# Full-height score products with masked queries, O normalised by DMA and the B branch in chunks, in a fused attention and MLP kernel

## Chip, cores, metric

One core of a Trainium2 chip. The metric is the device time of one execution in microseconds (us), and the number quoted for a kernel is the median of all its runs; ratios use fast runs alone. A run is called slow when it lies over 1.5% above the fastest of the same kernel. The kernel before varies; its profiled run took 1158.88 us, 8 us above its median.

## What is computed

A layer-normed input goes through attention with 32 heads of 20, and through a gated MLP branch (B). The two are multiplied, and the input is added.

```python
x  = A_x                                   # (1, 2048, 640) bf16
xn = layernorm(x)
# A: 32 heads, Dh = 20
q, k, v = split(xn @ wqkv)
s = softmax(q k^T / sqrt(20)) v @ wo
# B
h  = shift4(gelu(layernorm(xn) @ w1)) @ w2   # four column groups shifted by 1, -1, 2, -2 rows
x1 = xn + h
b  = x1 + gelu(layernorm(x1) @ w3) @ w4
out = x + s * silu(b)
```

## The kernel before

The program is a list of tasks with estimated durations. A static list scheduler (the "planner") simulates the engines with these estimates and writes one fixed order per engine. Afterwards every engine works its list strictly in order and waits on semaphores.

```python
self.dma_bw = 280.0          # planner: bytes per ns, shared by all DMAs
self.dma_lat0 = 1900.0       # planner: ns from issue to landing, plus bytes / dma_bw
...
t.start = st
t.finish = st + t.dur
if t.is_dma and t.nbytes:
    xs = max(t.finish, dma_free)
    dma_free = xs + t.nbytes / self.dma_bw
    t.lat = dma_free + self.dma_lat0 - t.finish
```

Attention works in "groups": four heads (a quad) times 512 queries, 32 groups in all. A head occupies 32 partitions. Scores of two heads are two *row tiles*, which stream side by side (in the trace of before the two of a pair start 3 ns apart, at 861.420 and 861.423 us, and take 385 ns each). ScalarE takes the exp of both (128x1024), and a product with V in four *column tiles* adds into one PSUM bank. Some key tiles are done by VectorE's own exp instead. Two 2-bank areas hold ScalarE's scores, one bank holds PV (the product with V; its row Z is the sum of the exps, by which the output is divided), and three further banks ("W") serve everything else: VectorE's scores, the B branch, projections and transposes.

```python
def score(e, out, i):                       # row tile: 21 of 128 rows
    return e.matmul(out, KT[32*i:32*i+21, b, 128*kt:128*kt+128], QT[32*i:32*i+21, b, q0:q0+512],
                    start=True, stop=True, tile_position=(32*i, 0))
# ... ScalarE's tiles
T("pe", 240, fn, ...); T("act", c_act(1024), ... e.activation(PT[:, slot, :], psum..., AF.Exp, scale=cfg.scale) ...)
# ... VectorE's tiles: scores into W banks
T("pe", 130, fn, reads=krd + qrd, writes=[wa, ("dseq",)], acq=("W", h))

def normalise(self, quad, qc):              # O^T sits in PSUM with Z in row 20 of each 32
    T("dve", ..., lambda e: e.transpose(Ot[:, :], self.bank(self.PVB)[:, :]))
    T("dve", ..., lambda e: e.reciprocal(RZ[:, ob, 0:16], Ot[:, 20:512:32]))
    T("dve", ..., fnn)                      # OnT = Ot * RZ, one factor per row and block of 32
    T("dve", ..., lambda e: e.transpose(OT[:, 512*qc:512*qc+512], OnT[:, ob, :]))

def run_b(self, quad):                      # the B branch is filler: TensorE takes it only
    self.cur_cls = 1                        # when nothing of attention is ready
    for want, stage in self.b_stages:
        if want == quad:
            stage()
    self.cur_cls = 0
```

## Time and profile before

| | before |
|---|---|
| time, median of 3 (range) | 1150.85 us (1143.3 to 1166.96) |
| first exp starts, last exp ends, end | 42.4, 1087.3, 1156.9 us |
| ScalarE busy / idle from first to last exp | 862.7 / 182.2 us |
| granted TensorE clock, mean | 0.816 |
| time at clock 0.50, summed over the trace | 427 us |

The profile is read in this order: ScalarE's exps are the largest block of work that cannot be given away, so the span is the time before the first exp (head), ScalarE's busy and idle time from first to last exp, and the time after it (tail). The busy shares, slices, stretches and the order of time stand in the prediction. What ScalarE waited for before the change (line waited for: us in total, times, longest us):

```profile
ACT arena L1087 <- PE psum L1071: 128.1, 201, 5.8
ACT arena L1383 <- DVE arena L1379: 41.9, 3, 24.0
ACT arena L1302 <- DVE arena L1296: 32.0, 1, 32.0
```

Between first and last exp stand the 201 small waits for score products and one large one, before a gelu (L1302), for VectorE's part of the B branch. The three before a silu (L1383) lie in the tail, but for 0.2 us. VectorE appears in no wait of an exp.

### The profile page before, as it was taken

The page shows a single profiled execution, that of the slowest core. Times are in us where ns is not written, and L with a number is a line of the kernel's source. Part 1 is how long each engine was busy: PE and PEld are TensorE (multiplying, and loading weights), DVE is VectorE, ACT ScalarE, POOL GpSimd, SP SyncE. Part 2 cuts the span into 40 slices and gives each one's busy share as a digit, 9 for nine tenths or more (in the row PEclk, how much of TensorE's full clock was granted, in tenths as well). Part 3 has the DMA queues.
Part 4 walks back from the last instruction along what each step waited for, and adds up shares of the span by engine and source line. Part 5 has one row for each costly group of instructions (what it writes and reads, how often), then busy time and mean ns, then how long its engine had stood idle before and what let it go on. Part 6 is the DMA issues. An engine that isn't in the chain of part 4 may idle for free.

```text
span 1156.9 us, 27991 instructions
## 1 busy us (share of the span) xinstructions
PE 1047.0 (90%) x12648; PEld 332.8 (29%) x12648; DVE 768.5 (66%) x1328; ACT 895.2 (77%) x914; POOL 30.8 (3%) x52
## 2 busy tenths in 40 slices
PE   4999999999779999999779999999989899989896
PEld 3422222222223332223221222123222233233374
DVE  6656677467447788676866687576787858843355
ACT  7589798688529899788847798688999989988700
POOL 3010000000000000000000000000010000000000
PEclk9978696598659899678855696587999889978999
DMA  4110000000110001000030001010021100200231
GB/s 114 10 32 6 1 5 5 2 1 1 9 43 2 2 2 8 2 2 1 5 85 1 7 13 20 13 29 2 1 48 41 25 2 19 47 7 8 52 117 59
DMA packets 85486, 24.53 MB, mean 21 GB/s; under 512 B 74360, under 2 KB 85368, under 8 KB 85368
## 3 DMA queue, kind: packets, MB, share of 16 engines
q1 hardware_dynamic: 85368, 22.75, 9.1%
q8 instruction: 99, 1.62, 0.6%
q14 instruction: 19, 0.16, 0.0%
HBM read 19.99 MB, written 2.62 MB: 20 GB/s over the span
## 4 chain that ended last, share of the span: by engine, by line
PE 74%; ACT 18%; DVE 5%; DMA 1%; issue 1%; POOL 0%; SPq 0%; DVEq 0%
PE psum L687 28%; PE psum L1071 25%; ACT arena L1087 15%; PE psum L1096 10%; PE psum L1144 9%; ACT arena L1370 1%; PE psum L908 1%; DVE arena L845 1%; DMA arena<-in_B_w_dram 1%; DVE arena L1296 1%; ACT arena L1383 1%; DVE arena L1121 1%; PE psum L944 0%; DVE arena L1227 0%; DMA arena<-in_A_x_dram 0%
## 5 line engine op out<-in xcount | busy, mean ns | idle before, releaser
L1087 ACT ACTIVATE arena<-psum 128x1024 bf16<-128x1024 f32 x844 | 818.4, 1028 | 155.6 <-PE psum L1071 128.1
L1071 PE MATMUL psum<-arena 21*128 21x512 bf16 x2048 | 419.5, 443 | 45.6 <-ACT arena L1087 37.3
L687 PE MATMUL psum<-arena 128*32 128x320 bf16 (+1 forms) x6480 | 421.4, 376 | 29.2 <-DVE arena L1296 7.5
L1134 DVE TENSOR_SCALAR arena<-arena 128x2048 uint16<-128x2048 uint16 x360 | 230.8, 689 | 42.0 <-PE psum L1144 40.8
L687 PEld LDWEIGHTS psum<-arena 128*32 128x32 bf16 x6480 | 161.7, 102 | 199.7 <-issue 84.3
L1124 DVE TENSOR_SCALAR arena<-psum 128x512 uint16<-128x512 f32 x266 | 170.4, 682 | 62.7 <-PE psum L1071 61.9
L1071 PEld LDWEIGHTS psum<-arena 21*128 21x128 bf16 x2048 | 91.7, 93 | 391.2 <-ACT arena L1087 224.5
L1096 PE MATMUL psum<-arena 128*22 128x512 bf16 x1688 | 191.1, 445 | 3.3 <-DVE arena L1158 3.3
L1144 PE MATMUL psum<-arena 128*22 128x512 bf16 x1440 | 135.5, 462 | 0.6 <-POOL arena L1048 0.6
L1096 PEld LDWEIGHTS psum<-arena 128*22 128x22 bf16 x1688 | 42.0, 90 | 128.2 <-issue 118.9
L1121 DVE TENSOR_SCALAR arena<-psum 128x1024 uint16<-128x1024 f32 x47 | 57.2, 1217 | 20.8 <-PE psum L1071 20.6
L1366 DVE CAST arena<-psum 128x512 bf16<-128x512 f32 x48 | 33.0, 689 | 41.3 <-PE psum L687 41.1
L1144 PEld LDWEIGHTS psum<-arena 128*22 128x22 bf16 x1440 | 36.8, 100 | 53.9 <-issue 41.7
L1383 ACT ACTIVATE arena<-arena 128x1280 bf16<-128x1280 bf16 x8 | 10.2, 1270 | 41.9 <-DVE arena L1379 41.9
L1158 DVE STREAM_TRANSPOSE arena<-psum 128x512 f32<-128x512 f32 x32 | 22.9, 715 | 24.9 <-PE psum L1096 24.5
L1296 DVE CAST arena<-psum 128x512 bf16<-128x512 f32 x20 | 13.8, 691 | 36.2 <-PE psum L687 36.2
L987 DVE TENSOR_SCALAR arena<-psum,arena 128x512 bf16<-128x512 f32 x32 | 23.7, 744 | 20.0 <-PE psum L687 19.9
L1379 DVE TENSOR_TENSOR arena<-psum,arena 128x320 bf16<-128x320 f32 x32 | 15.0, 488 | 32.6 <-PE psum L687 32.6
L908 PE MATMUL psum<-arena 128*32 128x128 bf16 x640 | 24.7, 276 | 10.1 <-DVE arena L918 5.8
L1302 ACT ACTIVATE arena<-arena 128x5120 bf16<-128x5120 bf16 x2 | 8.9, 4470 | 32.0 <-DVE arena L1296 32.0
L918 DVE COPY arena<-psum 128x512 bf16<-128x512 bf16 x40 | 16.8, 420 | 20.8 <-PE psum L908 20.7
L1327 DVE TENSOR_TENSOR arena<-psum,arena 128x320 bf16<-128x320 f32 x32 | 15.7, 489 | 19.6 <-PE psum L687 19.6
(70 smaller groups left out, 338.7 us busy)
## 6 DMA issues: line engine op xcount, KB each, us to landing
arena<-in_B_w_dram SPq DMA_DIRECT2D x48, 160.0 KB, 2.4
arena<-in_A_x_dram SPq DMA_DIRECT2D x8, 320.0 KB, 5.7
arena<-in_A_x_dram SPq DMA_DIRECT2D x16, 160.0 KB, 2.3
out_dram<-arena SPq DMA_DIRECT2D x16, 160.0 KB, 2.2
arena<-in_B_w_dram SPq DMA_DIRECT2D x1, 1920.0 KB, 8.3
arena<-in_A_wqkv_dram SPq DMA_DIRECT2D x64, 25.0 KB, 2.5
arena<-in_B_w_dram SPq DMA_DIRECT2D x2, 800.0 KB, 4.7
arena<-in_A_wqkv_dram SPq DMA_DIRECT2D x2, 400.0 KB, 6.5
```

The lines of the kernel that those rows point to most:

```text
L687: ins = e.matmul(pb[32 * c:32 * c + 32, 0:N], lhsT(k, c), rhs(k, c), start=(k == 0), stop=(k == nk - 1), tile_position=(0, 32 * c))
L908: ins = e.transpose(pb[32 * c:32 * c + 32, 128 * bi:128 * bi + 128], src_of(n)[:, kc * 128 + 32 * c: kc * 128 + 32 * c + 32], self.ident[: ...
L987: T("dve", c_dve(512), lambda e, h=h, c0=c0: e.tensor_scalar(KT[:, b, c0:c0 + 512], self.wbank(h)[:, 0:512], self.eaug[:, 0:1], None, op0= ...
L1071: return e.matmul(out, KT[32 * i:32 * i + 21, b, 128 * kt:128 * kt + 128], QT[32 * i:32 * i + 21, b, q0:q0 + 512], start=True, stop=True, ...
L1087: lambda e, sb=sb, slot=slot: e.activation(PT[:, slot, :], self.psum[:, 1024 * sb:1024 * sb + 1024], AF.Exp, scale=cfg.scale),
L1096: ins = e.matmul(pb[32 * i:32 * i + 22, 0:512], VA[:, ql, kt, i, :], PT[:, slots[i // 2], 512 * (i % 2):512 * (i % 2) + 512], start=first, ...
L1121: return e.tensor_scalar(dst, self.psum[:, 512 * (self.W0 + lo):512 * (self.W0 + hi + 1)], a_exp, EXP_BIAS, op0=ALU.mult, op1=ALU.add)
L1124: ins = e.tensor_scalar(dst[:, 512 * k:512 * k + 512], self.bank(self.W0 + s)[:, :], a_exp, EXP_BIAS, op0=ALU.mult, op1=ALU.add)
L1134: lambda e, s=s, v=v: e.tensor_scalar(SS[:, s, :], U[:, :], 0.5, EXP_B[v], op0=ALU.mult, op1=ALU.add),
L1144: ins = e.matmul(pb[32 * i:32 * i + 22, 0:512], w, SS[:, s, at:at + 512].bitcast(BF16), start=first and v == 0, stop=final and v == 3, til ...
L1296: T("dve", c_dve(512), lambda e, h=h, m=m, ch=ch: e.tensor_copy(hx[:, m, 512 * ch:512 * ch + 512], self.wbank(h)[:, 0:512]), reads=[wa], w ...
L1366: T("dve", c_dve(512), lambda e, h=h, fc=fc: e.tensor_copy(GT[:, fc, :], self.wbank(h)[:, 0:512]), reads=[wa], writes=at, name=f"gt_{ch}_{ ...
```

## The change

The intent: fewer switches between row tiles and column tiles on TensorE (about 0.10 us each from start to start in the kernel before) and a fuller array; less VectorE work in normalising; no B-branch rest after the last exp.

```diff
+# scores for ScalarE: four column tiles of 128 rows on queries that are zero outside one head
+T("sp", 240, lambda e: [e.dma_start(self.QM[32*i:32*i+32, gb, i, :], QT[32*i:32*i+32, b, 512*qc:512*qc+512]) for i in range(4)], ...)
+for c in range(4):
+    ins = e.matmul(bank[32*c:32*c+32, :], self.KT[:, b, 128*kt+32*c:128*kt+32*c+32],
+                   self.QM[:, gb, 2*a+jj, :], start=True, stop=True, tile_position=(0, 32*c))
+# row tiles stay in "blocks" of two key tiles that ScalarE and VectorE share: BLK = [(4,5),(9,10),(14,15)]
+# planner: a task has a tiling mode; a change costs 100 ns, and tasks of the same mode are taken first

 def normalise(self, quad, qc):
-    transpose, reciprocal, multiply, transpose          # four VectorE steps
+    T("dve", ..., lambda e: e.tensor_copy(Ob[:, :], self.bank(self.PVB)[:, :]))
+    T("sp", 240, fz, ..., ndma=4)      # Z: one row -> 32 partitions x 16, four heads
+    T("dve", ..., lambda e: e.reciprocal(RZ[:, ob, :], ZT[:, ob, :]))
+    T("sp", 240, fb, ..., ndma=4)      # 1/Z back into one row
+    T("sp", 240, fc, ..., ndma=4)      # that row to 19 further partitions: [[..],[0,19],[1,512]]
+    T("dve", ..., lambda e: e.tensor_tensor(dst, Ob[:, :], RB[:, :], op=ALU.mult))
+    T("sp", 60*len(moves), fd, ...)    # into O packed to 5 x 128 rows
+    # (the very last group keeps the transposes)

-# B branch: y2, w1, w2 over all 2048 rows, as filler (cls 1)
+# B branch: per chunk of 512 rows (y2 is its normalised input, RR the factor of each row), in the foreground (cls 0); ScalarE's scores get cls -1
+T("sp", 60, lambda e: e.dma_start(RR[1:128, :], bass.AP(..., [[..],[0,127],[1,S]])))   # row scale to 127 partitions
+T("dve", ..., fy)                      # y2 chunk = xnT * RR, waits for all of RR
```

Cut from the diff: row tiles of 32 rows instead of 21, bookkeeping for several DMAs under one semaphore, the tables of which group shares how many blocks, the output projection on five packed K tiles, memory layout. The planner has 60 ns for each DMA issue in all of it.

## The prediction

> **What bounds the kernel now.** I read the page's busy shares first, then its slices, then stretches, then the order of time at small scale, and last the waits.
>
> ```profile
> PE 1047.0 (90%) x12648; PEld 332.8 (29%) x12648; DVE 768.5 (66%) x1328; ACT 895.2 (77%) x914; POOL 30.8 (3%) x52
> ...
> PEclk9978696598659899678855696587999889978999
> ...
> L1087 ACT ACTIVATE arena<-psum 128x1024 bf16<-128x1024 f32 x844 | 818.4, 1028 | 155.6 <-PE psum L1071 128.1
> ```
>
> TensorE is busy 90% of the span, but its granted clock swings between 5 and 9 tenths. ScalarE, which must do 844 exps, sits idle 155.6 us in front of them, 128.1 us of that for the score products. So the question is why TensorE is late. Stretches (PE, PEld, DVE, ACT, POOL busy, then clock, DMA share, GB/s):
>
> ```profile
> 599.00:647.00 48.00, 46.69 (x360) 10.37 (x356) 31.36 (x62) 36.09 (x38) 1.11 (x2) 0.50 0.02 6
> 705.00:756.00 51.00, 50.25 (x344) 9.67 (x341) 27.53 (x44) 33.56 (x34) 0.00 (x0) 0.50 0.10 16
> 951.00:1018.00 67.00, 64.46 (x826) 20.11 (x826) 54.62 (x92) 64.10 (x67) 0.00 (x0) 1.00 0.14 31
> ...
> 42.40:1087.30 1044.90, 964.69 (x10524) 278.73 (x10523) 701.68 (x1164) 862.65 (x865) 20.73 (x20) 0.80 0.07 15
> 1087.30:1156.90 69.60, 56.82 (x1480) 38.26 (x1472) 37.79 (x80) 9.15 (x5) 0.00 (x0) 0.97 0.27 80
> ```
>
> The clock is 0.50 or 1.00, never between; means like 0.80 are mixtures. In a cold stretch ScalarE does 38 instructions in 48 us, or 34 in 51 us (1.26 and 1.5 us each); in the warm one 67 in 67 us (1.0). A mean of 0.80 over the 1045 us of attention is about 418 us cold. The first exp starts at 42.4 us, the last ends at 1087.3; after it come 70 us in which TensorE does 1480 matmuls left of the B branch and of the output projection. So there are two losses: cold clock, and a tail.
>
> Now the order of time. Cold, then warm:
>
> ```profile
> 602.77 0.61 PE L1071 MATMUL psum<-arena 21*128 21x512 bf16 x2
> 603.31 0.61 PE L1144 MATMUL psum<-arena 128*22 128x512 bf16 x4
> 603.71 0.54 PE L908 MATMUL psum<-arena 128*32 128x128 bf16 x12
> ```
> ```profile
> 861.42 0.39 PE L1071 MATMUL psum<-arena 21*128 21x512 bf16 x2
> 861.74 0.40 PE L1096 MATMUL psum<-arena 128*22 128x512 bf16 x4
> 861.96 0.58 PE L687 MATMUL psum<-arena 128*32 128x320 bf16 x12
> 862.47 0.39 PE L1071 MATMUL psum<-arena 21*128 21x512 bf16 x2
> ```
>
> Durations overlap, so take start to start. Warm: four column tiles of 512 (L1096) take 0.22 us. A pair of row tiles (L1071) takes 0.32 before column tiles follow, 0.10 more than its 0.216 of streaming. Twelve column matmuls of 320 followed by row tiles take 0.51: three passes of 0.135 and again 0.10. So each change of tiling costs 0.10 us, a round trip about 0.21. Cold, a pass takes 0.40 and the pair 0.54.
>
> [...]here 46.69 us busy of 48 stay at 0.50. I read this as: what counts is how much of the array works, and a row-tile pair lights 42 of 128 rows[...]. That is an inference. [...]
>
> **The change, part by part.** Counts are from the two programs' instruction orders.
>
> *Score products.* Of 2048 row-tile matmuls 712 stay. The other 1336 become 5344 full-height column matmuls on masked queries: two heads cost two passes, 0.432 us, instead of a pair at 0.216 plus up to 0.21 of switching. Runs of row tiles fall from 798 to 290. TensorE's work at full clock, before: 1450 passes of 512 at 0.216 = 313, 1024 row pairs = 221, 960 passes of 320 at 0.135 = 130, 960 transposes at about 0.029 = 28; 692, plus 798 x 0.21 = 168: 860 us. After: 2762 passes = 597, 356 pairs = 77, 896 passes of 320 = 121, 640 transposes = 19; 814, plus 290 x 0.21 = 61: 875 us. **So this saves no work at full clock.** What it buys is a fuller array: per key tile nearly four full-array passes and one of 22 of 32 columns, about 1.0 us of the 2 us that ScalarE needs. [...]
>
> *Exp.* Blocks shared with VectorE carry 82 key tiles' worth instead of 90, so ScalarE does 860 exps, 16 more. The unbroken run of 14 at 692 us took 13.15 us: (13.15 - 1.02)/13 = 0.933 each, 802 us. Gelu: 4 of 5.32, 4 of about 2.3 (half of the 4.47 of L1302), 8 silus of 1.27, 16 table loads of 1.28: about 61. ScalarE's floor between first and last exp is 863 us; TensorE's there is about 845 (875 less prologue and tail). Before, warm, ScalarE reached 95 to 96% busy (64.10 of 67). With TensorE as full as this I take 94%: 918 us, against 1045.
>
> *B branch in chunks, no longer mere filler.* All four last gelus now stand well before the last exp; after the last score come 64 matmuls, not the 1480. The end becomes PV, four VectorE steps (0.71, 0.24, 0.68, 0.70), eight last tiles and a 2.2 us store: about 12 us in place of 70. The prologue stays at 42. Sum so far: 42 + 918 + 12 = **972 us**.
>
> *Normalising by DMA.* Takes 2 of 4 VectorE steps away, some 23 us over 31 groups, none on the path. It adds, per group, four small DMAs for Z, four for 1/Z, four broadcasts of 19 rows of 2 KB. Issue costs 0.50 us each, as for today's small SBUF DMA (its line's instructions, then two rows of the DMA view: KB, us to landing):
>
> ```profile
> L1015 SPq DMA_DIRECT2D arena<-arena x32: 497/498/656, 39.6 to 858.0; - x32
> ```
> ```profile
> arena<-in_A_x_dram SPq DMA_DIRECT2D x16, 160.0 KB, 2.3
> arena<-in_B_w_dram SPq DMA_DIRECT2D x1, 1920.0 KB, 8.3
> ```
>
> Landing takes about 2.2 us, so four take about 3.7. The broadcasts, if on one engine: from the last two rows (10 and 120 KB per engine, 6 us apart) an engine moves about 19 GB/s, so 156 KB take 8.2 us, about 10 with the ends. From the copy out of PSUM to the last multiply that is about 17 us; VectorE's order has some 9 us of other work there, and it is in order. It stands about 8 us in each of 31 groups. TensorE notices when it needs a PSUM bank or a VectorE exp, after perhaps 5 us, and ScalarE 1 to 2 us later: 1.5 us a group, **45 us**.
>
> *The first chunk's row scale* is broadcast to 127 partitions, 1.04 MB. [...] VectorE's first y2 waits for it with about 4 us of work ahead of it; TensorE's order allows some 9 exps more. Lost once: about **30 us**.
>
> Masked-query DMAs (four of 32 KB a group, double buffered) are hidden: a group has nearly 27 us. Sum: 972 + 45 + 30 = 1047; **1040 us**, as one of the two waits may be smaller.
>
> **Rivals.**
> *A, all new DMA waits hidden:* the broadcasts spread over engines, or VectorE's third of idle time takes them up. For it: VectorE falls to about 700 us of busy. Against: it is in order. About 975 us.
> *B, VectorE's queue becomes the bound:* 700 us of work plus 31 x 8 of standing is 950, as much as ScalarE's; weight loads that SyncE issues between (2.06 us each for the 16 of the prologue) stretch the chain in some groups. For it: the schedule was made with issue costs of 60 ns. Then each group loses 4 us or more: 1100 to 1150.
> *C, the clock stays as it is:* masked rows are zeros, and if zeros don't count, TensorE's 875 at 0.8 is about 1090 with waits on top: 1110 to 1160. Against it: B-branch stretches of column tiles are warm in the trace.
>
> **Range and chances.** The 972 is sound within 30 us either way, except under C (1 in 10). New waits add 10 to 140. So 1040, with 975 to 1115 for 8 in 10. Faster by over 2% means under 1128: only B at its worst or C fail that. Faster 0.88, same 0.08, slower 0.04.
>
> **What would show it.** Clock between first and last exp at 0.93 or more. Start to start of column-tile scores 0.216 a pass. 860 exps with under 90 us of waiting. Last exp some 12 us before the end. A hole of about 30 us in ScalarE near 80 to 130 us, with VectorE waiting for a DMA at its first y2. VectorE waiting some 8 us for a DMA before each normalising multiply. Wrong if the clock stays near 0.8, if VectorE's DMA waits pass 350 us, or if the tail stays long.

## The result

**1253.28 us** median of 4 (1248.7 to 1263.23) against 1151.49 (1143.3 to 1166.96): ratio 1.0922, 95% interval 1.0812 to 1.1031. It is slower; the prediction was wrong (it had given slower a chance of 0.04). A ratio here is the mean time of one kernel's fast runs over that of the other's of the same rounds, so it is not quite the ratio of the medians quoted. (1.0922 comes out without before's 1166.96, which is 2.1% above its fastest.)

The page of the changed kernel, answering to the lines shown of before (busy us, share, instructions; clock slices; chain by engine; then groups: busy, mean ns | idle before, releaser):

```profile
PE 989.7 (79%) x15986; PEld 403.3 (32%) x15986; DVE 703.4 (56%) x1143; ACT 900.6 (72%) x937; POOL 30.4 (2%) x61
...
PEclk9986988889888888899988898898898889888897
...
PE 37%; DMA 27%; SPq 14%; DVE 12%; ACT 8%; issue 2%; ACTq 0%; DVEq 0%
...
L1200 ACT ACTIVATE arena<-psum 128x1024 bf16<-128x1024 f32 x860 | 817.2, 1035 | 327.9 <-PE psum L1193 209.5
...
L1287 DVE TENSOR_TENSOR arena<-arena 128x512 bf16<-128x512 f32 x31 | 21.5, 692 | 203.0 <-DMA arena<-arena 203.0
...
L1271 DVE RECIPROCAL arena<-arena 128x16 f32<-128x16 f32 x31 | 7.8, 251 | 41.5 <-DMA arena<-arena 41.5
L1442 DVE TENSOR_TENSOR arena<-arena 128x2570 bf16<-128x2570 bf16 (+1 forms) x4 | 11.3, 2833 | 34.1 <-DMA arena<-arena 34.1
```

No compute engine is anywhere near full. The chain names DMA with 27% and SyncE's queue with 14%. VectorE stands 203.0 + 41.5 + 34.1 = 278.6 us for DMAs (multiply, reciprocal, row scale). The stretches (PE, PEld, DVE, ACT, POOL busy, clock, DMA share, GB/s) give the account:

```profile
42.60:1243.90 1201.30, 962.90 (x15314) 386.57 (x15312) 664.82 (x1037) 877.07 (x892) 8.86 (x19) 0.89 0.11 26
1243.90:1255.60 11.70, 3.30 (x36) 0.88 (x36) 8.43 (x19) 0.02 (x1) 0.00 (x0) 0.63 0.33 108
79.60:114.10 34.50, 1.86 (x20) 0.79 (x24) 5.36 (x6) 0.04 (x1) 0.00 (x0) 0.55 0.06 22
```

From before to after the head is unchanged (42.4, 42.6), the tail falls by 57.9 us (69.6 to 11.7), and the stretch of exps grows by 156.4 (1044.9 to 1201.3): 14.4 more busy time on ScalarE and 142.0 more idle (182.2 to 324.2).

One group in the order of time, VectorE's stand and what it does to the others (start, us; in brackets the idle time before it and what ended it):

```profile
627.89 1.07 DVE L955 COPY arena<-psum 128x512 bf16<-128x512 bf16 x3
...
629.50 3.47 SPq L1284 DMA_DIRECT2D arena<-arena  x4
...
632.39 0.39 PE L1164 MATMUL psum<-arena 128*22 128x512 bf16 x4
637.57 0.69 DVE L1287 TENSOR_TENSOR arena<-arena 128x512 bf16<-128x512 f32 x1 [8.60 <-DMA arena<-arena]
638.18 1.28 DVE L1228 TENSOR_SCALAR arena<-psum 128x512 uint16<-128x512 f32 x2
...
639.52 0.62 PE L722 MATMUL psum<-arena 128*32 128x512 bf16 x4 [6.73 <-DVE arena L1228]
```
```profile
613.25 20.48 ACT L1200 ACTIVATE arena<-psum 128x1024 bf16<-128x1024 f32 x22 [0.52 <-PE psum L1193]
641.04 1.02 ACT L1200 ACTIVATE arena<-psum 128x1024 bf16<-128x1024 f32 x1 [7.31 <-PE psum L1193]
```

VectorE comes to the multiply (L1287) at 628.96. The broadcasts are only being issued from 629.50, four issues in 3.47 us, and the last one lands before 637.57. Behind the multiply in VectorE's list stands the exp L1228, which holds the W banks that TensorE's next tile needs: TensorE goes dry at 632.78, ScalarE at 633.73, 4.8 us after VectorE. But the restart is nearly as slow as the run-down: multiply, two exps, a tile, a score. ScalarE resumes 3.5 us after VectorE. Of 8.60 us of standing ScalarE loses 7.31. The two exps behind the multiply did not pass it: their scores were computed at 629.53 and 630.51 us, and they started at 638.18, after the multiply.

### The profile page after: what moved, and what is told of

Same layout as the page of the kernel before. It is cut to its first block, busy times and chain, and to the rows that moved or that the text cites. A ratio compares the mean times of both kernels' runs of the same rounds, so it can differ in the third digit from the quotient of the medians.

```text
span 1255.6 us, 35173 instructions
## 1 busy us (share of the span) xinstructions
PE 989.7 (79%) x15986; PEld 403.3 (32%) x15986; DVE 703.4 (56%) x1143; ACT 900.6 (72%) x937; POOL 30.4 (2%) x61
## 3 DMA queue, kind: packets, MB, share of 16 engines
q1 hardware_dynamic: 109480, 35.62, 12.2%
## 4 chain that ended last, share of the span: by engine, by line
PE 37%; DMA 27%; SPq 14%; DVE 12%; ACT 8%; issue 2%; ACTq 0%; DVEq 0%
DMA arena<-arena 26%; PE psum L722 13%; PE psum L1193 12%; ACT arena L1200 7%; SPq L1284 5%; PE psum L1175 4%; PE psum L1164 4%; SPq L1276 4%; SPq L1268 3%; DVE arena L1225 2%; PE psum L1153 2%; DVE arena L1138 2%; DVE arena L1287 1%; DMA arena<-in_B_w_dram 1%; DVE arena L882 1%
## 5 line engine op out<-in xcount | busy, mean ns | idle before, releaser
L1200 ACT ACTIVATE arena<-psum 128x1024 bf16<-128x1024 f32 x860 | 817.2, 1035 | 327.9 <-PE psum L1193 209.5
L722 PE MATMUL psum<-arena 128*32 128x320 bf16 (+1 forms) x6224 | 399.1, 356 | 75.1 <-DMA arena<-in_B_w_dram 16.3
L1193 PE MATMUL psum<-arena 128*32 128x512 bf16 x5344 | 441.7, 410 | 11.6 <-ACT arena L1200 9.1
L722 PEld LDWEIGHTS psum<-arena 128*32 128x32 bf16 x6224 | 166.1, 101 | 247.8 <-issue 54.9
L1175 PE MATMUL psum<-arena 32*128 32x512 bf16 x712 | 137.9, 410 | 99.1 <-DVE arena L1225 53.8
L1138 DVE TENSOR_SCALAR arena<-arena 128x2048 uint16<-128x2048 uint16 x328 | 208.5, 687 | 7.4 <-PE psum L1153 5.9
L1193 PEld LDWEIGHTS psum<-arena 128*32 128x32 bf16 x5344 | 122.3, 101 | 178.7 <-ACT arena L1200 108.8
L1164 PE MATMUL psum<-arena 128*22 128x512 bf16 x1720 | 172.7, 404 | 1.2 <-ACT arena L1200 1.2
L1225 DVE TENSOR_SCALAR arena<-psum 128x1024 uint16<-128x1024 f32 x114 | 138.6, 1216 | 43.4 <-PE psum L1175 42.3
L1153 PE MATMUL psum<-arena 128*22 128x512 bf16 x1312 | 119.6, 402 | 37.1 <-DVE arena L1138 36.8
L1287 DVE TENSOR_TENSOR arena<-arena 128x512 bf16<-128x512 f32 x31 | 21.5, 692 | 203.0 <-DMA arena<-arena 203.0
L1175 PEld LDWEIGHTS psum<-arena 32*128 32x128 bf16 x712 | 31.1, 92 | 222.2 <-DVE arena L1225 70.1
L1228 DVE TENSOR_SCALAR arena<-psum 128x512 uint16<-128x512 f32 x100 | 63.9, 680 | 20.1 <-PE psum L1175 19.6
L1508 DVE CAST arena<-psum 128x512 bf16<-128x512 f32 x48 | 32.9, 687 | 44.5 <-PE psum L722 44.4
L1521 DVE TENSOR_TENSOR arena<-psum,arena 128x320 bf16<-128x320 f32 x32 | 15.2, 488 | 42.6 <-PE psum L722 42.6
L1271 DVE RECIPROCAL arena<-arena 128x16 f32<-128x16 f32 x31 | 7.8, 251 | 41.5 <-DMA arena<-arena 41.5
L1442 DVE TENSOR_TENSOR arena<-arena 128x2570 bf16<-128x2570 bf16 (+1 forms) x4 | 11.3, 2833 | 34.1 <-DMA arena<-arena 34.1
L1372 DVE SCALAR_TENSOR_TENSOR arena<-psum,arena 128x320 bf16<-128x320 f32 x32 | 15.1, 486 | 26.7 <-PE psum L722 26.7
L1467 DVE TENSOR_TENSOR arena<-psum,arena 128x320 bf16<-128x320 f32 x32 | 15.6, 487 | 17.5 <-PE psum L722 17.3
```

The source lines that it names most:

```text
L722: ins = e.matmul(pb[32 * c:32 * c + 32, 0:N], lhsT(k, c), rhs(k, c), start=(k == 0), stop=(k == nk - 1), tile_position=(0, 32 * c))
L1138: lambda e, s=s, v=v: e.tensor_scalar(SS[:, s, :], U[:, :], 0.5, EXP_B[v], op0=ALU.mult, op1=ALU.add),
L1153: ins = e.matmul(pb[32 * i:32 * i + 22, 0:512], w, SS[:, s, at:at + 512].bitcast(BF16), start=False, stop=final, tile_position=(0, 32 * i))
L1164: ins = e.matmul(pb[32 * i:32 * i + 22, 0:512], VA[:, ql, kts[i // 2], i, :], PT[:, slots[i // 2], 512 * (i % 2):512 * (i % 2) + 512], sta ...
L1175: return e.matmul(out, self.KT[32 * i:32 * i + 32, b, 128 * kt:128 * kt + 128], self.QT[32 * i:32 * i + 32, b, 512 * qc:512 * qc + 512], s ...
L1193: ins = e.matmul(self.bank(2 * sb + jj)[32 * c:32 * c + 32, :], self.KT[:, b, 128 * kt + 32 * c:128 * kt + 32 * c + 32], self.QM[:, gb, 2 ...
```

## The experiments

Twelve kernels ran, all with the right result. Each ratio is against the kernel before on the same chip. The record's own class for each of the twelve is "unclear" (three rounds each); the 95% intervals below are what is compared, and only e15's comes within 2% of 1. Edits are against the changed kernel unless another is named. Their line numbers differ by a few lines.

| run | time, us | ratio (95%) | clock | at 0.50, us | ScalarE idle, first to last exp, us |
|---|---|---|---|---|---|
| before | 1151.49 | 1 | 0.816 | 427 | 182 |
| after | 1253.28 | 1.0922 (1.0812 to 1.1031) | 0.888 | 284 | 324 |
| e4 broadcast to 32 rows | 1291.27 | 1.1238 (1.1196 to 1.1280) | 0.881 | 309 | 355 |
| e8 row scale in 8 DMAs | 1257.91 | 1.0952 (1.0907 to 1.0997) | 0.891 | 274 | 322 |
| e2 steps on GpSimd | 1184.29 | 1.0303 (1.0259 to 1.0347) | 0.910 | 215 | 261 |
| e10 chain wholly on GpSimd | 1067.73 | 0.9322 (0.9259 to 0.9385) | 0.953 | 103 | 145 |
| e5 transposes | 1013.07 | 0.8829 (0.8772 to 0.8886) | 0.977 | 49 | 90 |
| e16 plan with measured costs | 1023.97 | 0.8934 (0.8823 to 0.9044) | 0.974 | 56 | 100 |
| e12 e5 + row tiles | 1005.54 | 0.8748 (0.8651 to 0.8844) | 0.951 | 99 | 74 |
| e13 e5 + B as filler | 1092.81 | 0.9544 (0.9464 to 0.9624) | 0.961 | 86 | 169 |
| e15 e5 + both | 1099.72 | 0.9532 (0.9232 to 0.9832) | 0.901 | 220 | 179 |
| e11 e5 + row scale in chunks | 988.50 | 0.8626 (0.8567 to 0.8685) | 0.987 | 27 | 65 |
| e14 e11 + row tiles | 984.32 | 0.8587 (0.8450 to 0.8725) | 0.940 | 121 | 66 |
| e17 e16 + row scale in chunks | 992.47 | 0.8639 (0.8591 to 0.8687) | 0.987 | 28 | 70 |

The clock and the last two columns are from the profiled run alone.

### e4: is it the number of DMA engines?

The edit broadcasts to 32 rows instead of 19, to spread each broadcast over the DMA engines. It changes two things at once: the spread, and the bytes, by 68%.

```diff
 ra: 1/Z back into one row
-  RB[32*i:32*i+1]                          (first row of the target)
+  Ob[32*i+31:32*i+32]                      (a spare partition)
 rb: broadcast
-  RB[32*i+1:32*i+20]  <- [[..],[0,19],[1,512]]
+  RB[32*i:32*i+32]    <- [[..],[0,32],[1,512]]
```

> The changed kernel with its 1/Z row kept in a spare partition and broadcast to 32 rows instead of 19, so that each broadcast can spread over the DMA engines; the orders of TensorE, VectorE, ScalarE and GpSimd are the same. Theory (VectorE's in-order wait for the broadcasts is handed on in full): from the first broadcast's issue to the multiply 8.1 us falls to some 4.3 (four issues of 0.69 and 1.7 to land), the wait before the multiply from 203 us in 31 to about 85, and the time by as much, 1253 to about 1138. Rival (TensorE's doubled score passes are the bound, and VectorE's waits lie beside them): within 2% of 1253. [...]

Measured 1291.27 us: missed. The order of the compute engines is that of the changed kernel, and the multiply waits longer:

```profile
L1287 DVE TENSOR_TENSOR arena<-arena 128x512 bf16<-128x512 f32 x31 | 21.5, 692 | 233.7 <-DMA arena<-arena 233.7
```

In one group four broadcasts of 64 KB are issued from 644.81 us and the multiply starts at 653.79, 9.0 us for 256 KB; in the changed kernel it is 8.1 us for 152 KB (629.50 to 637.57). The spread is there: while the broadcasts run, 0.06 of sixteen engines are busy in the changed kernel (630.8 to 637.2 us), that is one, and 0.70 here (646.0 to 653.4); over the whole span the packets' share of sixteen engines goes from 12.2% to 23.5%. And the spread does gain rate, 35 GB/s instead of 24, but the 68% more bytes use it up. So e4 does not show by itself that the number of engines is no limit; e8, where the bytes stay the same, does for the row scale. The same 19 rows cut into DMAs of 16 and 3, which would keep the bytes, were not run. The run gives one thing more: 30.7 us of additional standing at the multiply (203.0 to 233.7; 33.6 us with the reciprocal) made the span 30.8 us longer (1255.6 to 1286.4), and the medians differ by 38.0. **VectorE's standing passes to the span nearly in full.**

### e8: the row scale in eight DMAs

```diff
-one DMA:    RR[1:128, :]  <- row 0                        (127 rows)
+eight DMAs: RR[1:16], RR[16:32], ... RR[112:128] <- row 0  (16 rows each, the first 15)
```

> The changed kernel with the one broadcast of 8 KB rows to 127 partitions cut into eight of 16 (one of 15) partitions; compute orders the same. Theory: the single wait of 34.1 us at the first y2 shrinks to under 5 us and the time by 30, to about 1222. If the hole in ScalarE had another cause: no change.

Measured 1257.91 us: missed. VectorE's wait for the row scale, before here and in the changed kernel, is 32.9 and 34.1 us:

```profile
L1447 DVE TENSOR_TENSOR arena<-arena 128x2570 bf16<-128x2570 bf16 (+1 forms) x4 | 11.3, 2833 | 32.9 <-DMA arena<-arena 32.9
```

From the issue at 68.0 us to the first y2 at 108.74 in the changed kernel it is 40.7 us for 1.04 MB, 25.6 GB/s. While the data come, 0.07 of sixteen engines are busy in the changed kernel (69.33 to 108.25 us) and 0.96 in e8 (71.01 to 109.29; on its page 7 and 4 tenths in the two slices from 62.6 to 125.2 us, where the changed kernel has 0 and 0), and both move 28 GB/s in all. Some fifteen engines are no faster than one here. What limits both was not shown.

### e2: both waiting steps on GpSimd

```diff
-T("dve", ..., e.reciprocal(RZ, ZT))          ; T("dve", ..., e.tensor_tensor(dst, Ob, RB, op=mult))
+T("pool", 3400, e.tensor_tensor(RZ, ZT, M1, op=pow))   # M1 = -1
+T("pool", c_pool(512), e.tensor_tensor(dst, Ob, RB, op=mult))
```

> The changed kernel with the reciprocal (as a power of -1) and the normalising multiply moved from VectorE to GpSimd, which is 98% idle: the DMA chain stays as long, but nothing that TensorE needs stands behind it. Theory: 203 + 41 us of waits leave VectorE and the time falls to 1010 to 1040. Rival (the length of the DMA chain itself matters, for the PSUM bank or the output): still above 1200. Rival (TensorE bound by the full-height products): 1150 or more.

Measured 1184.29 us: 69 us less than the changed kernel, and far from what I expected. VectorE now waits for no DMA of the chain. But SyncE issues the chain's DMAs, and it too is in order. Its waits, then TensorE's:

```profile
SPq L1304 <- POOL arena L1289: 140.9, 27, 6.3
SPq L1278 <- POOL arena L1273: 140.8, 30, 24.8
```
```profile
PE psum L722 <- DMA arena<-in_B_w_dram: 71.2, 12, 20.7
```

SyncE stands 140.8 us before the issue that follows the reciprocal and 140.9 us before the one that follows the multiply. Behind these stand the loads of B's weights, which arrive late: 71.2 us of TensorE in 12 waits. In one place SyncE issues a weight at 599.37 us, TensorE has waited 20.70 us for it at 601.94, and ScalarE 21.48 at 603.46. The wait was moved from one in-order queue to another.

### e10: the chain's DMAs issued from GpSimd too

```diff
 (on top of e2)
-T("sp", 240, fz / fb / fc ...), T("sp", 60*len(moves), fd ...)
+T("pool", 240, fz / fb / fc ...), T("pool", 60*len(moves), fd ...)
```

> As e2 (reciprocal and multiply on GpSimd), but the whole chain's DMAs (Z, 1/Z, broadcast, O) are issued from GpSimd too, so that SyncE's in-order queue holds no load of weights behind them. Theory (the wait moved in e2 from VectorE's order to SyncE's order): the holes of 13 to 21 us, in which TensorE waits for weights that SyncE has not issued, go, and the time falls from 1184 to 1010 to 1050. Rival (the DMA chain is slow for the kernel whoever waits): above 1150.

Measured 1067.73 us, 117 us less than e2. TensorE's waits for weights fall from 71.2 to 6.1 us, which confirms the reading of e2: what stood on SyncE, not the loads themselves, cost this. It ends a little above the expected range. 38.1 us of ScalarE's 145 us of idle are the row-scale hole; some 50 us in places of 6 to 10 us are left that I didn't trace.

### e5: normalising by transposes, the rest of the change kept

```diff
-copy, z DMA, reciprocal, ra DMA, rb DMA, multiply      (31 groups)
+transpose, reciprocal, multiply, transpose             (as before; od DMA into packed O kept)
```

> The changed kernel with the normalisation of before (two VectorE transposes, reciprocal, multiply), only the result moved by DMA into the packed O: that part of the change undone, all else kept. Theory: the 244 us of waits go, 31 x 0.7 us of VectorE work come: 1010 to 1050, faster than before. Rival (another part of the change is what costs): stays above 1150.

Measured 1013.07 us: expected, and 240 us less than the changed kernel. So the whole loss, and more, sits in the normalising part. The clock is 0.977 and the last exp is followed by 11.1 us. VectorE's remaining large DMA wait is 34.6 us for the row scale.

### e16: the changed kernel, planned with measured costs

This leaves every task, every DMA and every buffer, and alters only the planner's estimates. One by-product: VectorE's exp over two W banks is one instruction where the plan puts the banks side by side and two where it doesn't, 114 and 100 instructions in the changed kernel, 99 and 130 here (1143 and 1158 in all).

```diff
-T("sp", 240, fz / fb ...)                                T("sp", 240, <masked queries>)
+T("sp", 2400, fz / fb ...)                               T("sp", 2400, <masked queries>)
-T("sp", 240, fc, ..., nbytes=128*2048)                   # broadcasts
+T("sp", 2740, fc, ..., lat=5300)
-T("sp", 60*len(moves), fd)      T("sp", 60, <W3 load>)   <row scale> nbytes=1048576
+T("sp", 700*len(moves), fd)     T("sp", 430, <W3 load>)  <row scale> lat=38000
```

Cut: two further groups of four DMAs (the loads of wqkv, a small row of Q) go from 240 to 2100.

> The changed kernel with every instruction, DMA and buffer as it is; only the estimates that the static scheduler plans with are set to what the trace of the changed kernel shows: issuing four small DMAs takes SyncE 2.1 to 2.7 us instead of 0.24, a 430 ns weight issue instead of 60, the four broadcasts land 5.3 us after their issue, the row-scale broadcast 38 us. So VectorE's list puts the reciprocal and the multiply later. Theory (the loss is a place in an in-order list, fixed with wrong DMA times): VectorE's waits for DMA fall from 203 + 41.5 + 34 us to under 80 in sum, the clock rises to 0.94 or more, 1030 to 1090 us. Rival (the DMA chain is too slow wherever the multiply stands, because SyncE's queue or the buffers behind it then wait): still 1180 us or more.

Measured **1023.97 us**, better than expected and 229 us less than the changed kernel with the same tasks:

```profile
PEclk9997899999999999998999999999999999999998
...
L1200 ACT ACTIVATE arena<-psum 128x1024 bf16<-128x1024 f32 x860 | 806.0, 1036 | 105.2 <-PE psum L1164 54.4
...
L1287 DVE TENSOR_TENSOR arena<-arena 128x512 bf16<-128x512 f32 x31 | 21.3, 687 | 9.6 <-DMA arena<-arena 9.5
L1271 DVE RECIPROCAL arena<-arena 128x16 f32<-128x16 f32 x31 | 7.6, 246 | 28.9 <-DMA arena<-arena 28.9
```

The multiply's wait is 9.5 us instead of 203.0. **The chain is no faster:** from the copy out of PSUM to the multiply the median is 18.2 us in the changed kernel's trace and 20.3 here. What differs is what stands between them in VectorE's list. One group (VectorE alone; the copy is L1262):

```profile
569.54 0.68 DVE L1262 COPY arena<-psum 128x512 f32<-128x512 f32 x1
...
587.28 1.23 DVE L1225 TENSOR_SCALAR arena<-psum 128x1024 uint16<-128x1024 f32 x1 [1.04 <-PE psum L1175]
588.42 0.68 DVE L1287 TENSOR_TENSOR arena<-arena 128x512 bf16<-128x512 f32 x1
```

The multiply has no idle time in front of it: it comes 18.9 us after the copy, when the data are there. The planner's own figures say the same: with its old costs it put the multiply 11.9 us after the copy on average, with the measured ones 20.5. Both plans end at about the same time in the planner's view (982.5 and 987.1 us); only the second is nearly what the chip does. The multiply could only be placed as late as the estimates said: 203.0 against 9.5 us of waiting. As the plan was made anew, other engines' orders moved as well, and no run moves the multiply alone; but TensorE's wait for B's weights fell only from 16.3 to 7.1 us, while VectorE's three DMA waits fell by 240.2 us (278.6 to 38.4) and the span by 234.7 (1255.6 to 1020.9), 0.98 of it.

Of the reciprocal's 28.9 us, 25.7 are a single wait, and its cause is on SyncE (start, us; x4 are four issues):

```profile
70.97 29.70 SPq L1003 DMA_DIRECT2D arena<-in_A_wqkv_dram  x4
100.72 2.45 SPq L1268 DMA_DIRECT2D arena<-arena  x4
```

The row-scale broadcast had been issued at 60.13, and its last packet ended at 100.43. Four small weight loads, issued behind it, took 29.70 us to issue, until 100.67 (in the changed kernel's trace four from this line take 2.10, at 131.79), and the first group's Z (L1268) behind those came at 100.72. So while the large broadcast ran, the issues behind it in SyncE's queue were held up. The changed kernel shows the same, with Z right behind it: 17.78 us for four issues, where 2.4 is usual.

```profile
68.00 0.69 SPq L1419 DMA_DIRECT2D arena<-arena  x1
72.04 17.78 SPq L1268 DMA_DIRECT2D arena<-arena  x4
```

### e12, e13, e15: what keeps the clock up?

These three tested the other half of my prediction, on e5 as it has no normalising chain. e12 makes all scores row tiles again (no masked queries). They are not quite those of before: the change also widened a row tile from 21 rows to 32 (21*128 in before's page, 32*128 in e12's), so a pair spans 64 of 128 rows and not 42. e13 makes the B branch filler again. e15 does both.

```diff
 e12: -col = self.grp > 0          +col = False
 e13: -self.cur_cls = 0            +self.cur_cls = 1      (in run_b)
 e15: both
```

> As e5, but all score products stay row tiles, as before the change. Theory (full-height products hold the clock up, and save no work): row-tile runs 822 instead of 285, clock from 0.977 to 0.80 to 0.90, cold spells of tens of us, time 1060 to 1120. Rival (the schedule of the B branch and the tail made the gain): clock may fall but the time stays within 2% of 1013.

> As e5, but the B branch is again work of the second class that fills holes, as before the change. Theory (the tail is what its schedule bought): the end after the last exp grows from 11 us to 50 or 70, the time to 1040 to 1080, the clock stays at 0.95 or more. Rival (the order of the B branch matters for the clock too): clock under 0.93.

> The fourth corner: transposes for the normalisation (as in e5), all scores row tiles (as in e12), and the B branch as second-class filler (as in e13). Either of the two alone kept the clock at 0.95 to 0.96. Theory (the clock needs stretches full of column tiles nearby; full-height scores or a spread B branch each give them): with both away the clock falls to 0.80 to 0.87 and the time is 1120 to 1180, about the kernel before. Rival (something else in the change, such as scores grouped by tiling mode or the shared blocks, holds the clock): clock 0.93 or more, 1070 to 1100 us.

e12 missed: 1005.54 us, no worse than e5's 1013.07. Without full-height products the clock falls from 0.977 to 0.951 (0.931 to 0.951 over e12's four runs; the profiled one is the fastest), and nothing is lost by it. e13 came out at 1092.81, just above its range. It costs 80 us, but not after the last exp, as I had written (that tail is 14 us): the late gelus and silus, which ScalarE must do in order between the exps, wait for the B branch (ScalarE's waits):

```profile
ACT arena L1482 <- DVE arena L1478: 56.2, 3, 22.9
ACT arena L1495 <- DVE arena L1491: 54.2, 6, 10.2
```

e15 is between the two theories: clock 0.901, which neither had, and 1099.72 us (1096.73 without its slow run), which is the rival's. So with the B branch as filler the row tiles do leave more cold time (220 us against e13's 86), but the time is the same within the intervals (0.9532 and 0.9544). What costs is the filler: 1013 to 1093 with full-height scores, 1006 to 1100 with row tiles. The clock is a poor guide to it: e13 has 0.961 and takes 1093, e12 0.951 and takes 1006.

Between e15 and the kernel before some 50 us are left (by the interval 19 to 88, as only two of before's seven runs beside it were fast). ScalarE's idle time from first to last exp is the same (179 and 182 us); the tail is 14.2 instead of 69.6. Which of the remaining parts (two chunked stages, scheduling by tiling mode, shared blocks, wider row tiles, packed O) does this, and which of them brings the cold time from 427 to 220 us, no run tells apart.

### e11, e14: the best versions

```diff
 e11 (on e5): row scale in four DMAs of 512 columns, one semaphore each; y2 of a chunk waits for the two that it reads
 e14 (on e11): col = False (all scores row tiles)
```

> As e5 (normalised by transposes), and the row scale broadcast in four column chunks with a semaphore each, so that the first y2 needs 258 KB of it, not 1.04 MB. From e8: cutting it by partitions left the wait at 32.9 us[...], about 27 GB/s. Theory: first chunk lands after about 10 us and 2 of latency, the wait of 34.6 us falls to 5 to 9 and the time from 1013 to about 986. Rival (VectorE waits for all four because they share engines): 1013.

> Candidate for the best version: transposes for the normalisation, the row scale broadcast in four chunks, all scores row tiles, the B branch in the foreground: e11 without full-height products and masked queries. e12 took 1005.5 with a 41 us hole for the row scale; without about 26 us of it: 970 to 990 us, at or below e11's 988.5. Rival (full-height products do hold the clock once the hole that hid it is gone): 1000 us or more, clock under 0.95.

e11 measured 988.50 us, as expected. Its first y2 waits 8.0 us instead of 34.6. The columns come in the order in which they are needed. e14 measured 984.32, inside its range. It isn't told apart from e11 (0.8587 and 0.8626, intervals that overlap). With 121 us at half clock against e11's 27, ScalarE idles as little (66 and 65 us). The exps on e14's page:

```profile
L1199 ACT ACTIVATE arena<-psum 128x1024 bf16<-128x1024 f32 x860 | 805.2, 1060 | 67.6 <-PE psum L1174 46.1
```

The masked queries, their 124 DMAs and 4008 matmuls (15986 against 11978) could go.

### e17: the changed kernel's normalising, without its two holes

```diff
 (on e16)
+row scale in four chunks, as e11 (planned at 9.5 us each)
+the first group is normalised by transposes: its Z would stand behind the broadcast
```

> e16_plan_costs (normalising by DMA, measured costs in the plan) with its last hole taken away: the row scale goes out in four chunks with a semaphore each, as in e11, and the very first group is normalised by transposes, because in e16 its Z waited 25.7 us for SyncE, which stood behind the broadcast. Theory (with the multiply well placed, normalising by DMA costs nothing): e16's 1024 less its 24.6 us hole, plus about 5 left of it: 995 to 1010 us, VectorE's waits for DMA before multiply and reciprocal under 20 us in sum. The further claim, that the two VectorE steps it saves are worth something: below e11's 988 us. I expect the first and not the second, for VectorE is not the bound. Rival (DMA normalising has a price of its own besides waits, such as SyncE's late issue of weights): 1010 us or more.

Measured 992.47 us: a little better than expected, and not below e11's 988.50 (0.8639 and 0.8626). VectorE's waits for multiply and reciprocal are 16.0 + 7.2 us, slightly over the 20 I gave:

```profile
DVE arena L1291 <- DMA arena<-arena: 16.0, 15, 2.3
...
DVE arena L1275 <- DMA arena<-arena: 7.2, 9, 1.7
```

I take both claims as held: well placed, normalising by DMA costs nothing that these runs can tell, and the two VectorE steps that it saves are worth nothing, as VectorE (708.6 us busy of 991.0) isn't the limit. But e17 was planned with the measured costs and e11 with the old ones, and e11 under the measured costs was not run, so the two differ in more than the normalising.

## Why the prediction was wrong, step by step

Its sum beside the trace of the changed kernel:

| term | predicted, us | measured, us |
|---|---|---|
| head | 42 | 42.6 |
| exps and ScalarE's other work, ordinary gaps | 918 | 943 (877.1 busy, 66 of other idle) |
| row-scale hole | 30 | 34.5 |
| VectorE standing for the chain, what reaches ScalarE | 45 | 224 |
| tail | 12 | 11.7 |
| sum | 1047, given as 1040 | 1255.6 |

The measured 224 is ScalarE's idle time in the windows from the start of each of VectorE's stands to 6 us after its end, each moment counted once: 203.3 at the 31 multiplies, 20.4 more at the 25 reciprocals that stood. The 66 are what is left of 324.2 after the hole. The 6 us are a choice: with 4 it would be 196, with 8 it would be 243. (In e16 the windows at the multiplies hold 22 us where hardly anything stands, so up to about that much of the 203 would be there anyway.)

**The step that failed:** "TensorE notices when it needs a PSUM bank or a VectorE exp, after perhaps 5 us, and ScalarE 1 to 2 us later: 1.5 us a group, 45 us." The standing itself was sized well: 8 us in each of 31 groups is 248, and the trace has 203.0 + 41.5 = 244.5. (In part by luck: the chain took 17.5 us from the copy's end to the multiply, median of 31, where 17 was written, but an issue took 0.59 to 0.69 us and not 0.50, a landing 1.7 and not 2.2, and one engine moved 24 GB/s in the broadcasts and not 19.) Also right was that it is the issues and broadcasts against "some 9 us of other work". Wrong was what passes on: not 0.19 but nearly all, 224 us of 244.5 by these windows. e4 shows it with 33.6 us more standing and 30.8 more span, e16 with 240.2 less and 234.7 less. I had subtracted the time that the engines take to run dry. They take nearly as long to fill again (4.8 us to run dry and 3.5 to fill in the group shown), so a stand on the path shifts everything behind it by its length. And VectorE was on the path, though only 56% busy, because its next item held the banks.

**Rival B** was this outcome in kind: VectorE's queue the bound, "the schedule was made with issue costs of 60 ns". I gave it 1100 to 1150 and too little weight. It was also a warning that I didn't follow to its end: if the plan is the fault, then the plan's place for the multiply is what to check, and e16 shows that the plan's costs alone are worth 229 us. Rival A (about 975) is what the change gives once the waits are hidden: e17 has 992.

**The clock.** Predicted at 0.93 or more between first and last exp, measured 0.89 there. The cause ran the other way round. In the changed kernel TensorE has 28 gaps of over 3 us between matmuls, 182 us in all, and 26 of its 37 cold spells (at 0.50) begin at one; nearly all spells last 3.4, 6.8 or 10.2 us. The standing made the clock fall, not the reverse: with the waits gone it is 0.977 (e5) and 0.974 (e16). My reading that a fuller array holds the clock was an inference, and no run shows it: e12 keeps 0.951 with row tiles, and e14 is as fast as e11 at 0.940. It isn't refuted either, for these row tiles have 32 rows where those of before have 21, and no run took the old ones. **Rival C** isn't tested by this in itself, but e5 with masked rows runs at 0.977, so zeros don't keep the clock down.

**The engine count.** I took the broadcasts as slow because they run on one engine. They do (0.06 and 0.07 of sixteen busy), and the size came out right (a wait of 34.1 us for the row scale, against 30), but for the row scale the cause did not: on some fifteen engines (e8) it took as long, a wait of 32.9 us. For the group's broadcasts e4 leaves it open. The 30 us were my estimate, and no trace of the kernel before shows the rate that they took for one engine; here one engine moved the 1.04 MB at 26.7 GB/s.

**What held.** 860 exps; 0.216 us a pass of column-tile scores at full clock; the head; the tail (57.9 us gained); the row-scale hole (34.5 us); no work saved at full clock by full-height products, which e12 and e14 show as no time saved; 918 for the exps' stretch without waits (in e11 it is 931). What did not, besides the sum: "under 90 us of waiting" before the exps, where 327.9 were measured.

**What stays open.** Which parts of the change besides the B branch in the foreground bring the kernel before to e15's time; why the clock of the kernel before stays at 0.50 for 48 us on end with TensorE 46.69 us busy; why row tiles with B as filler leave 220 us cold and full-height ones 86; the rest of e10's waits; and what limits a broadcast from one partition.

## What to carry to other kernels

In a list that an engine works in order, what matters is where the waiting item stands, not how fast its data come: give the planner the measured time of issue and landing of every DMA, and the wait can cost next to nothing, as in e17; guess them too low and each one can stop everything behind it, as here. Count such a stand in full when the next item in the list feeds the bottleneck, for here the engines refilled nearly as slowly as they ran dry (3.5 us against 4.8), and a low busy share of the standing engine is no comfort. Moving a wait to another in-order queue only asks the same question again there (SyncE stood 140.8 and 140.9 us in e2, GpSimd 241.5 us for the chain's DMAs in e10).
